# Seven instead of six gate tiles in the first phase of a fused LayerNorm, SSM and SwiGLU kernel, with its transposes through one PSUM bank

## The chip, the cores and the metric

The kernel runs on one core of one Trainium2 chip. The metric is the device time of one execution in microseconds (us); lower is better. A run of the kernel before takes about 180 us.

Engine names follow the profile: PE is TensorE, ACT is ScalarE, DVE is VectorE, POOL is GpSimd, SP is SyncE. ACTq and SPq are the sequencers of ScalarE and SyncE when they issue DMA loads. Times of a profile are counted from the start of its span. The span is about 1.7 us shorter than the device time.

## The reference, cut to what matters

The input is 2048 tokens of 512 bf16 values. They are layer-normalised; the result goes through a linear recurrence (the SSM part) and through a SwiGLU block with 1376 hidden columns; both are added to the input.

```python
def _layernorm(x, axis=-1, eps=1e-5):
    m = jnp.mean(x, axis=axis, keepdims=True)
    v = jnp.var(x, axis=axis, keepdims=True)
    return (x - m) / jnp.sqrt(v + eps)

def _B_ref(x, w_gate, w_up, w_down):        # w_gate, w_up: 512 x 1376
    g = _silu(x @ w_gate)
    u = x @ w_up
    return (g * u) @ w_down

xn = _layernorm(x, axis=-1)
return x + _A_ref(xn, ...) + _B_ref(xn, w_gate, w_up, w_down)   # _A_ref: the recurrence; cut
```

The hidden columns make ten full tiles of 128 and a rest of 96. Tokens are taken in four chunks of 512; a chunk is four token tiles of 128.

## The kernel before: the parts that matter

The kernel records each operation as a task with its reads and writes. A list scheduler puts the tasks into one fixed order for each engine, and semaphores are placed from the dependencies. Every engine then works through its order strictly in sequence. Keep that in mind: a computing instruction that waits holds up those behind it on its engine (VectorE's wait of 0.77 us in the profile after is the case that matters here).

The loads. `x_load(a)` brings one token tile (128 KB). `wg_load` brings gate weights: a0 holds rows 0 to 255 of the weight, a1 and a2 the next 128 rows each, and each of them only the columns that the first phase needs (`FH0`, six tiles). The loads a0 and a1 are issued by ScalarE, behind a tiny one (`ld_touch`, 0.2 KB); all others are issued by SyncE.

```python
FH0 = 6 * 128
def wg_load(nm, k0, k1, **kw):
    return dma("ld_wg" + nm, wg[:, k0:k1, 0:FH0], wg_v[:, k0:k1, 0:FH0], [("wg", nm)], ...)

x_load(0)
x_load(1)
act_q = [dma("ld_touch", ..., eng="act")]
act_q.append(wg_load("a0", 0, 2, eng="act", order=(act_q[-1],)))
x_load(2)
act_q.append(wg_load("a1", 2, 3, eng="act", order=(act_q[-1],)))
wg_load("a2", 3, 4)
x_load(3)
# ... parameters, the rest of the weights, token tiles 4 to 7
```

The layer norm of the first four token tiles, on VectorE except for one square root per tile on ScalarE.

```python
def ln_chunk0():
    last = ln_stat0(0, (bn_full(0),))
    last = bn_half(1, 0, order=(last,))           # statistics of tile 1, first half
    for a in range(4):
        last = g.add("dve", ... reciprocal of sd0[a] ..., order=(last,))
        for h in range(2):
            last = ln_half(a, h, order=(last,))   # normalised token tile, halves of 256
        if a < 3:
            last = bn_half(a + 1, 1, order=(last,))
            last = ln_stat0(a + 1, (last,))
        if a < 2:
            last = bn_half(a + 2, 0, order=(last,))
```

The transposes and the gate matmuls. A normalised half tile is transposed on PE into PSUM, the memory that PE writes its results to (two transposes). ScalarE then evacuates it, that is, copies it out to SBUF, the memory that PE reads, as `xnT`. In the kernel before, the two halves of a tile use the two banks of one PSUM pair, and six gate tiles use three more pairs, so all eight banks are taken. The gate matmuls of this phase have only 128 tokens each ("quarter matmuls").

```python
def xt_tile_fine(a, hs=(0, 1)):
    for h in hs:
        slot = xt_pair[0] + h                     # one bank for each half
        # PE: two transposes of xn_sb[:, a, half h] into ptr[:, slot, 0:256];
        #     with a == 3, h == 1 also that of 12 rows of parameters
        # ACT: evacuation to xnT[:, 0, a, 2h:2h+2, :]

def ffn_gate_quarters(pairs):                     # pairs = [0, 1, 2]: six gate tiles
    xt_pair[0] = next_pair()
    banks = {ip: next_pair() for ip in pairs}
    tiles = [(2 * ip + k, banks[ip] + k) for ip in pairs for k in range(2)]
    pe_warm(...)                                  # matmuls on constants
    ln_chunk0()
    # ... transposes of tile 0
    for q in range(4):                            # the four token tiles
        # ... for each gate tile 4 quarter matmuls (contraction 4 x 128);
        #     the transposes of tile q + 1 in between
    act_table(AF.Silu, (hold["evac"],))           # an activation that loads the Silu table
    for ip in pairs:
        silu_pair(0, ip, banks[ip])               # ACT, two gate tiles at a time
```

After the phase, PE goes on with matmuls of 512 tokens: `ffn_up(0, 0)` to `ffn_up(0, 2)`, then the gate tiles 6 to 9, and so on.

## Time and profile before

| kernel before | value | view of the profile |
|---|---|---|
| device time | 179.89 us, median of 3 runs (179.84 to 180.25) | list of runs |
| span | 178.2 us | page |
| first gate matmul | 5.89 us | timeline of PE |
| first up matmul, start of the 512-token stream | 12.65 us | timeline of PE |
| PE idle between these two ("holes") | 0.67 us | start-to-start distances of PE's instructions above 56 ns |
| token tile 1 landed | 3.96 us | last completion record of its load |

These are two lines of the page. The first gives busy time, share of the span and instructions of each engine, the second the chain of waits that ended last, by engine:

```profile
PE 174.2 (98%) x918; PEld 83.5 (47%) x926; DVE 162.0 (91%) x278; ACT 89.4 (50%) x117; POOL 9.6 (5%) x21
PE 95%; DMA 1%; DVE 1%; issue 1%; ACT 0%
```

PE is busy nearly all the time and is nearly all of the chain. This change can't make a busy PE faster, since it adds no gate work and removes none. It can only gain where PE idles, and that is in the first 12.65 us.

This is the timeline of PE in the phase (start in us, busy us, engine, line of the kernel, operation, output and inputs, shapes, count; in brackets idle time before it and what ended it):

```profile
5.89 1.17 PE L786 MATMUL pb<-xnT,wg 128*128 128x128 bf16 x18 [0.17 <-ACT xnT L571]
6.89 0.28 PE L565 MATMUL pb<-ident,xn_sb 128*128 128x128 bf16 x2
7.00 0.33 PE L786 MATMUL pb<-xnT,wg 128*128 128x128 bf16 x3
7.17 0.28 PE L565 MATMUL pb<-ident,xn_sb 128*128 128x128 bf16 x2
7.28 1.20 PE L786 MATMUL pb<-xnT,wg 128*128 128x128 bf16 x15
8.45 0.28 PE L565 MATMUL pb<-ident,xn_sb 128*128 128x128 bf16 x2
...
12.65 0.59 PE L738 MATMUL pb<-xnT,wu 128*128 128x512 bf16 x2
```

L786 are the quarter matmuls, L565 the transposes. Busy times overlap, since matmuls are pipelined; use the starts. From 7.28 to 8.45 there are 1.17 us for 15 matmuls, which at 56 ns take 0.84 us: here PE idles 0.33 us although the lines show no wait: 0.19 us of it is inside the group, before the matmul at 7.64 us, and 0.13 us between its last matmul and the transposes at 8.45 us.

The following lines are VectorE's timeline at the start:

```profile
3.09 0.69 DVE L525 BATCH_NORM_STATS2 st<-x_sb 128x6 f32<-128x512 bf16 x1 [3.09 <-DMA x_sb<-in_A_x_dram]
3.81 0.18 DVE L517 BATCH_NORM_AGGREGATE mv<-st 128x2 f32<-128x6 f32 x1
3.99 0.43 DVE L507 BATCH_NORM_STATS2 st<-x_sb 128x6 f32<-128x256 bf16 x1
4.36 0.16 DVE L529 RECIPROCAL rstd<-sd 128x1 f32<-128x1 f32 x1
4.56 0.60 DVE L512 TENSOR_SCALAR xn_sb<-x_sb,mv,rstd 128x256 bf16<-128x256 bf16 x2
```

ScalarE's end of the phase is its load of the Silu table and then the silus:

```profile
11.53 1.28 ACT L461 ACT_TABLE_LOAD   x1
12.83 0.29 ACT L461 ACTIVATE sm<-epst 128x1 f32<-128x1 f32 x1
13.03 2.83 ACT L750 ACTIVATE sg<-pb 128x1024 bf16<-128x1024 f32 x3
```

The last view of before is that of the DMA issues in the first 12 us: output and source, sequencer, count, KB of one, and the median time from issue to landing in us.

```profile
x_sb<-in_A_x_dram SPq DMA_DIRECT2D x4, 128.0 KB, 3.3
wg<-in_B_w_gate_dram ACTq DMA_DIRECT2D x1, 384.0 KB, 3.6
```

### The profile page before, as it was taken

What the parts mean: (1) busy time and instruction counts of PE and PEld (TensorE: products, weight loads), DVE (VectorE), ACT (ScalarE), POOL (GpSimd) and SP (SyncE); (2) the same over time, 40 slices, a digit from 0 to 9 for tenths busy, and PEclk for the clock granted to TensorE, in tenths of its full rate; (3) what the DMA queues carried; (4) which work ended last, traced back from release to release, by engine and by line L of the source; (5) the groups of instructions that cost most, each with busy time, mean ns of one, the idle gap of its engine ahead of it and who ended that gap; (6) DMA issues with size and microseconds to landing.
All of it is one profiled execution on the core that took longest, in us unless ns stands there. A gap on an engine that the chain in (4) does not pass through costs nothing.

```text
span 178.2 us, 2394 instructions
## 1 busy us (share of the span) xinstructions
PE 174.2 (98%) x918; PEld 83.5 (47%) x926; DVE 162.0 (91%) x278; ACT 89.4 (50%) x117; POOL 9.6 (5%) x21
## 2 busy tenths in 40 slices
PE   8999999999999999999999999999999999999994
PEld 3784444444444444444444444444444444444743
DVE  2959983889799999999999999999999999999983
ACT  4479989999799948016565651000965620000000
POOL 3033100002200000040000000000000000000000
PEclk9999999999999999999999999999999999999999
DMA  5995569459360000002420000001100000000122
GB/s 170 364 339 117 120 118 115 97 169 346 95 118 4 0 0 0 0 18 72 95 56 0 0 0 4 0 0 59 58 0 4 0 0 0 0 0 4 59 86 91
DMA packets 22979, 12.37 MB, mean 69 GB/s; under 512 B 15193, under 2 KB 22969, under 8 KB 22969
## 3 DMA queue, kind: packets, MB, share of 16 engines
q1 hardware_dynamic: 22472, 11.64, 24.7%
q10 hardware_dynamic: 496, 0.59, 1.0%
q8 instruction: 7, 0.11, 0.3%
q14 instruction: 4, 0.02, 0.0%
HBM read 6.46 MB, written 2.10 MB: 48 GB/s over the span
## 4 chain that ended last, share of the span: by engine, by line
PE 95%; DMA 1%; DVE 1%; issue 1%; ACT 0%
PE pb L738 36%; PE pb L938 21%; PE pb L855 16%; PE pb L951 15%; PE pb L786 3%; PE pb L818 2%; DMA x_sb<-in_A_x_dram 1%; PE pb L828 1%; PE pb L565 1%; DVE st L525 0%; DVE st L507 0%; ACT xnT L571 0%; DVE xn_sb L512 0%; DVE x_sb L956 0%; DVE mv L517 0%
## 5 line engine op out<-in xcount | busy, mean ns | idle before, releaser
L895 DVE TENSOR_TENSOR_SCAN rot<-sm,car,rot 128x512 bf16<-128x512 f32 x32 | 39.0, 1266 | 0.1
L938 PE MATMUL pb<-wd,hT 128*128 128x512 bf16 (+3 forms) x194 | 38.1, 355 | 0.2
L738 PE MATMUL pb<-xnT,wu 128*128 128x512 bf16 x160 | 37.3, 379 | 0.0
L738 PE MATMUL pb<-xnT,wg 128*128 128x512 bf16 x136 | 32.0, 379 | 0.0
L951 PE MATMUL pb<-W,hss 128*128 128x512 bf16 (+2 forms) x140 | 28.1, 355 | 0.2
L855 PE MATMUL pb<-xnT,BT 128*128 128x512 bf16 x128 | 28.1, 379 | 0.0
L938 PEld LDWEIGHTS pb<-wd,hT 128*128 128x128 bf16 (+1 forms) x198 | 18.5, 98 | 19.9
L738 PEld LDWEIGHTS pb<-xnT,wu 128*128 128x128 bf16 x160 | 15.5, 98 | 18.8 <-ACT uf L808 0.4
L808 ACT ACTIVATE uf<-pb 128x1024 bf16<-128x1024 f32 x20 | 20.4, 1027 | 7.0 <-PE pb L738 6.2
L750 ACT ACTIVATE sg<-pb 128x1024 bf16<-128x1024 f32 x20 | 20.2, 1023 | 7.3 <-PE pb L738 7.3
L738 PEld LDWEIGHTS pb<-xnT,wg 128*128 128x128 bf16 x136 | 13.1, 98 | 16.4 <-issue 0.8
L951 PEld LDWEIGHTS pb<-W,hss 128*128 128x128 bf16 x144 | 13.5, 98 | 14.3
L855 PEld LDWEIGHTS pb<-xnT,BT 128*128 128x128 bf16 x128 | 12.5, 98 | 15.1
L862 ACT ACTIVATE u_sb<-pb 128x1024 bf16<-128x1024 f32 x16 | 16.4, 1026 | 4.6 <-PE pb L855 4.2
L810 DVE TENSOR_TENSOR hT<-sg,uf 128x1024 bf16<-128x1024 bf16 x20 | 13.5, 682 | 1.0 <-ACT uf L808 0.8
L886 DVE TENSOR_TENSOR rot<-u_sb,cosT 128x2048 bf16<-128x2048 bf16 x8 | 9.7, 1217 | 2.9 <-ACT cosT L699 2.9
L956 DVE TENSOR_TENSOR x_sb<-pb,x_sb 128x512 bf16<-128x512 f32 (+2 forms) x18 | 10.8, 622 | 1.4 <-PE pb L951 1.4
L837 ACT ACTIVATE sg<-pb 96x1024 bf16<-96x1024 f32 x2 | 2.0, 1020 | 17.3 <-PE pb L818 17.3
L501 ACT ACTIVATE xn_sb<-x_sb,nmr,rstd 128x512 bf16<-128x512 bf16 x8 | 5.9, 804 | 9.5 <-DVE nmr L498 9.5
L886 DVE TENSOR_TENSOR rot<-rot,cosT 128x2048 bf16<-128x2048 bf16 x8 | 9.7, 1216 | 0.1
L886 DVE TENSOR_TENSOR rot<-rot,sin 128x2048 bf16<-128x2048 bf16 x8 | 9.7, 1217 | 0.0
L886 DVE TENSOR_TENSOR rot<-u_sb,sin 128x2048 bf16<-128x2048 bf16 x8 | 9.7, 1215 | 0.0
(77 smaller groups left out, 141.2 us busy)
## 6 DMA issues: line engine op xcount, KB each, us to landing
out_dram<-x_sb SPq DMA_DIRECT2D x15, 128.0 KB, 1.7
x_sb<-in_A_x_dram SPq DMA_DIRECT2D x3, 512.0 KB, 7.6
wd<-in_B_w_down_dram SPq DMA_DIRECT2D x1, 1280.0 KB, 7.1
wu<-in_B_w_up_dram SPq DMA_DIRECT2D x1, 768.0 KB, 4.8
wg<-in_B_w_gate_dram SPq DMA_DIRECT2D x1, 608.0 KB, 6.2
wu<-in_B_w_up_dram SPq DMA_DIRECT2D x1, 608.0 KB, 7.3
x_sb<-in_A_x_dram SPq DMA_DIRECT2D x4, 128.0 KB, 3.3
wg<-in_B_w_gate_dram ACTq DMA_DIRECT2D x1, 384.0 KB, 3.6
```

What stands on the lines that cost most here:

```text
L501: g.add("act", lambda e, a=a: e.activation(out=xn_sb[:, a % NXN, :], in_=x_sb[:, a, :], func=AF.Identity, scale=rstd[:, a:a + 1], bias=nmr ...
L738: inst = e.matmul(pbank[0:fs, bk, :].rearrange("p (j t) -> p j t", j=4), lhsT=w[:, kt, i * 128:i * 128 + fs], rhs=xnT[:, c % 2, :, kt, :], ...
L750: g.add("act", lambda e: e.activation(out=sg[rows, sl, 0:n, :].rearrange("p a t -> p (a t)"), in_=pair_f32(rows, bk, 512 * n), func=AF.Sil ...
L808: g.add("act", lambda e: e.activation(out=uf[rows, ul, 0:n, :].rearrange("p a t -> p (a t)"), in_=pair_f32(rows, bk, 512 * n), func=AF.Ide ...
L810: g.add("dve", lambda e: e.tensor_tensor(out=hT[rows, hb, i0:i0 + n, :], in0=sg[rows, sl, 0:n, :], in1=uf[rows, ul, 0:n, :], op=ALU.mult), ...
L855: inst = e.matmul(pbank[:, bk, :].rearrange("p (j t) -> p j t", j=4), lhsT=BT[:, ri, kt, pt * 128:(pt + 1) * 128], rhs=xnT[:, c % 2, :, kt ...
L862: g.add("act", lambda e: e.activation(out=u_sb[:, us].rearrange("p r t -> p (r t)"), in_=pair_f32(slice(0, 128), b0), func=AF.Identity), r ...
L886: tt = lambda out, a, b, op, r, w, nm: g.add("dve", lambda e: e.tensor_tensor(out=out, in0=a, in1=b, op=op), reads=r, writes=w, name="%s_% ...
L895: g.add("dve", lambda e, A0=A0, A1=A1, k=k, ri=ri, pt=pt: e.tensor_tensor_scan(out=A1[:, k, ri, :], data0=rr[:, pt:pt + 1].to_broadcast([1 ...
L938: inst = e.matmul(pbank[:, bk, 0:nc_], lhsT=hT[0:fs, hb, i, lt * 128:(lt + 1) * 128], rhs=wd[0:fs, i, c0:c0 + nc_], start=(i == 0), stop=F ...
L951: inst = e.matmul(pbank[:, bk, 0:nc_], lhsT=hss[:, hb, pt, ri, lt * 128:(lt + 1) * 128], rhs=W12[:, ri, pt, c0:c0 + nc_], start=False, sto ...
L956: g.add("dve", lambda e, bk=bk, a=a, c0=c0, nc_=nc_: e.tensor_tensor(out=x_sb[:, a, c0:c0 + nc_], in0=pbank[:, bk, 0:nc_], in1=x_sb[:, a, ...
```

## The change

The intent is to fill PE's holes. VectorE needs about 1.74 us for the layer norm of a token tile, while PE's share for it is 24 quarter matmuls and 4 transposes, 28 x 56 ns = 1.57 us. With a seventh gate tile it is 32 x 56 ns = 1.79 us. The seventh tile needs a PSUM bank, so both halves of a tile's transposes now share one bank, and an eighth gate tile, made with 512-token matmuls, takes that bank at the end. The four silus then have all eight banks, and the first up matmul must wait for the first silu. So that it needn't wait long, token tile 3 is evacuated by VectorE, and ScalarE loads its Silu table earlier. The gate loads ahead of the phase grow from 768 to 896 columns, 128 KB in all. The diff, cut to its core:

```diff
         FH0 = 6 * 128
+        NQ = 7
+        FG = NQ * 128
@@ wg_load and ld_wg1
-    return dma("ld_wg" + nm, wg[:, k0:k1, 0:FH0], wg_v[:, k0:k1, 0:FH0], ...)
+    return dma("ld_wg" + nm, wg[:, k0:k1, 0:FG], wg_v[:, k0:k1, 0:FG], ...)
-        dma("ld_wg1", wg[:, :, FH0:Fh], wg_v[:, :, FH0:Fh], ...)
+        dma("ld_wg1", wg[:, :, FG:Fh], wg_v[:, :, FG:Fh], ...)
@@ ln_chunk0: order on VectorE
-                for h in range(2):
-                    last = ln_half(a, h, order=(last,))
+                last = ln_half(a, 0, order=(last,))
                 if a < 3:
                     last = bn_half(a + 1, 1, order=(last,))
                     last = ln_stat0(a + 1, (last,))
+                last = ln_half(a, 1, order=(last,))
                 if a < 2:
                     last = bn_half(a + 2, 0, order=(last,))
@@ xt_tile_fine: one bank, tile 3 evacuated by VectorE
-                slot = xt_pair[0] + h
+            slot = xt_pair[0]
...
+            if a == 3:
+                t = g.add("dve", lambda e: e.tensor_copy(out=dst, in_=src), ..., order=(hold["xn3"],))
+                if par:
+                    g.add("dve", lambda e: e.tensor_copy(out=praw..., in_=ptr[:, slot, 512:524]), ..., order=(t,))
+            else:
+                t = g.add("act", lambda e: e.activation(out=dst, in_=src, func=AF.Identity), ...)
@@ ffn_gate_quarters
-            xt_pair[0] = next_pair()
             banks = {ip: next_pair() for ip in pairs}
+            xt_pair[0] = tiles.pop()[1]
...
+                for k0, k1 in ((0, 2), (2, 3), (3, 4)) if q == 0 else ((0, 2), (2, 4)):
+                    if k0 == 2 and q < 3:
+                        xt_tile_fine(q + 1, 0)
+                    for i, bk in tiles:
+                        # ... quarter matmuls k0 to k1 of gate tile i
+                if q < 3:
+                    xt_tile_fine(q + 1, 1)
...
+            seq = ["sd0", "ev00", "sd1", "ev01", "ev10", "sd2", "ev11", "sd3", "ev20", "ev21"]
+            # ... this order is fixed on ScalarE
-            act_table(AF.Silu, (hold["evac"],))
+            act_table(AF.Silu, (hold["ev21"],))
+            ffn_mm(0, NQ, "g", xt_pair[0])
@@ order of the first chunk
-        ffn_gate_quarters([0, 1, 2])
+        ffn_gate_quarters([0, 1, 2, 3])
...
-        for ip in range(3, 5):
-            ffn_gate(0, ip)
+        ffn_gate(0, 4)
```

## The prediction

> **What bounds the kernel.** TensorE. The page gives PE 174.2 of 178.2 us (98%), and 95% of the chain that ended last is PE; the granted clock is 1.0. Read one by one, matmuls of 512 columns start 216 ns apart, those of 128 columns 56 ns apart. This agrees with the Trainium skill, "TensorE: Matmul & The Clock Gate", section "Wait — 56ns, not 53.3ns?" (55.6 and 215.7 ns warm). From 12.65 us, where the 512-column stream starts, to the last matmul I find no wait beyond places where records are missing. VectorE is busy 91%, but off the chain.
>
> So the only time to win is before 12.65 us. The timeline of PE between the first gate matmul (5.89) and 12.65 shows holes: 0.19 us at 7.6, 0.13 at 8.4, 0.17 at 10.2, 0.15 around the parameter transpose at 10.6; sum 0.63. The cause is VectorE: one token tile of layernorm takes it 1.74 us (xn tiles start at 4.56, 6.30, 8.04, 9.78), while PE's share for six gate tiles is 24 matmuls and 4 transposes, 28 x 56 ns = 1.57 us.
>
> **What the change does.**
> - A seventh gate tile makes PE's share 32 x 56 ns = 1.79 us: 16 added quarter matmuls (0.89 us) partly fill the holes, and four 512-column matmuls (0.86 us) go later. PE work in total is unchanged; only filled holes count. Ceiling: 0.63 - 0.15 (parameters stay), about 0.45 us.
> - One transpose bank costs a round trip. In before, from a transpose to the first matmul after its evacuation is 0.75 us (6.89 to 7.64). Between transposes stand 14 matmuls, 0.78 us, so this mostly fits. At the start it doesn't: the second half's transpose waits for the first evacuation, and the first gate matmul comes at about 6.0, 0.1 later.
> - The fourth square root is ordered before tile 2's first evacuation on ScalarE and waits for its statistics: about 0.15 us of PE idle.
> - 128 KB more gate weight is loaded ahead of the tokens. At the 371-389 GB/s of the windows this delays token tile 2 (landed 5.57, needed at 5.66) by an estimated 0.2, hence the statistics by 0.1-0.15.
> - The early Silu table load (1.28 us, measured) and two evacuations on VectorE free ScalarE: the first silu (before: 13.03) needs only tile 1's last matmul, about 12.8-13.0. All eight banks hold gate tiles, so the first up matmul must wait for that silu (1.0 us): ready at about 14.1, when tile 7's 512-column matmuls (0.86 us) end at 14.1-14.3.
>
> Sum: up starts at about 14.2, against 12.65 + 8 x 0.216 = 14.37 with two gate tiles counted ahead. Gain 0.2 us, all on the critical path. The last VectorE scan result lands 0.35 us before PE uses it (168.4 against 168.74), which caps a gain near 0.35.
>
> **Prediction: 179.68 us, range 179.30 to 180.10; faster by over 2% 0.01, same 0.98, slower 0.01.**
>
> **What will show it.** Timeline of PE: first quarter matmul at 6.0; tile 7's 512-column matmuls from about 13.3; first up matmul 14.1-14.3; holes in the phase below 0.45 us; PE unbroken after. ScalarE: table load at about 10.4, four silus in a row from 13.0.
>
> **What would make it wrong.** The first up matmul waiting over 0.2 us on the silu; a late token tile; a hole at every single-bank transpose; PE waiting for VectorE at the last hss, which would hide a larger gain.

## The result, and the profile after

| | before, same rounds | after |
|---|---|---|
| median device time | 180.07 us (179.84 to 180.46, 6 runs) | 180.19 us (179.72 to 180.32, 6 runs) |
| ratio after/before | | 1.000, 95% interval 0.9982 to 1.0018: same |
| span of the profiled run | 178.2 us | 178.6 us |
| first gate matmul | 5.89 us | 6.75 us |
| from it to the first up matmul | 6.76 us | 8.09 us |
| first up matmul | 12.65 us | 14.84 us |
| holes in between | 0.67 us | 0.26 us |
| token tile 1 landed | 3.96 us | 4.76 us |

Ratios lie within 0.001 of the ratio of the mean times of the same rounds (`after_one_ring` excepted), and aren't quite the ratio of the medians that are quoted. The kernel before itself took 180.07 us in these rounds; at the time of the prediction 179.89 us was known. The profiled run of after took 180.30 us, the profiled one of before 179.93 us; the two traces therefore show one of after's longer runs beside one of before's shorter runs, and their difference of 0.37 us in span is larger than that of the kernels.

The page's line of busy time for the kernel after; PE is still the busiest, a little less so over a longer span:

```profile
PE 173.3 (97%) x929; PEld 83.9 (47%) x937; DVE 162.3 (91%) x281; ACT 88.7 (50%) x114; POOL 9.9 (6%) x21
```

The timeline of PE in the phase, L780 being the quarter matmuls and L739 the 512-token matmuls:

```profile
5.80 0.27 PE L565 MATMUL pb<-ident,xn_sb 128*128 128x128 bf16 x2 [1.41 <-DVE xn_sb L514]
5.91 0.49 PE L474 MATMUL pb<-const-bfloat16-1.0 128*128 128x256 bf16 x3
6.63 0.27 PE L565 MATMUL pb<-ident,xn_sb 128*128 128x128 bf16 x2 [0.23 <-ACT xnT L577]
6.75 0.94 PE L780 MATMUL pb<-xnT,wg 128*128 128x128 bf16 x14
7.53 0.28 PE L565 MATMUL pb<-ident,xn_sb 128*128 128x128 bf16 x2
7.64 0.94 PE L780 MATMUL pb<-xnT,wg 128*128 128x128 bf16 x14
8.42 0.27 PE L565 MATMUL pb<-ident,xn_sb 128*128 128x128 bf16 x2
...
13.98 1.03 PE L739 MATMUL pb<-xnT,wg 128*128 128x512 bf16 x4
14.84 1.46 PE L739 MATMUL pb<-xnT,wu 128*128 128x512 bf16 x6
```

Now the transposes come every 0.89 us (6.63, 7.53, 8.42), and 14 matmuls and 2 transposes at 56 ns are 0.896 us. PE has no holes here; the aim of the change is met. Two gate tiles more now come before the first up matmul: sixteen quarter matmuls, which are as much work as four matmuls of 512 tokens, and the four of tile 7. Counted as eight matmuls of 512 tokens they cost 8 x 0.216 = 1.73 us that before has to do later. So the stretch from first gate to first up takes 8.09 - 1.73 = 6.36 us against 6.76 us: the change wins 0.40 us there.

But the phase begins 0.86 us later. VectorE's timeline tells why:

```profile
3.10 0.69 DVE L527 BATCH_NORM_STATS2 st<-x_sb 128x6 f32<-128x512 bf16 x1 [3.10 <-DMA x_sb<-in_A_x_dram]
3.83 0.18 DVE L519 BATCH_NORM_AGGREGATE mv<-st 128x2 f32<-128x6 f32 x1
4.78 0.43 DVE L509 BATCH_NORM_STATS2 st<-x_sb 128x6 f32<-128x256 bf16 x1 [0.77 <-DMA x_sb<-in_A_x_dram]
5.12 0.15 DVE L531 RECIPROCAL rstd<-sd 128x1 f32<-128x1 f32 x1
5.31 0.35 DVE L514 TENSOR_SCALAR xn_sb<-x_sb,mv,rstd 128x256 bf16<-128x256 bf16 x1
```

Token tile 0 is there as early as before (3.10 against 3.09). Then VectorE waits 0.77 us for token tile 1, whose first-half statistics stand in its order ahead of tile 0's reciprocal. The tile that PE needs next is held up by one that it needs 1.7 us later (PE transposes them at 5.80 and 7.53 us). The view of DMA issues has the same (median of four token tiles 4.1 instead of 3.3 us):

```profile
x_sb<-in_A_x_dram SPq DMA_DIRECT2D x4, 128.0 KB, 4.1
wg<-in_B_w_gate_dram ACTq DMA_DIRECT2D x1, 448.0 KB, 4.5
```

The completion records of that load add a detail: a load here ends with 16 updates, as many as the core has DMA engines. For token tile 1, fifteen of them were in at 4.17 us in the kernel after, and the sixteenth came at 4.76 us; in the five loads that landed next, the last update again came 0.45 to 0.70 us behind the fifteenth. This looks like one late DMA engine, but the records don't name the engine. In the kernel before, the last two updates came at 3.92 and 3.96 us.

ScalarE's end of the phase:

```profile
11.01 1.28 ACT L463 ACT_TABLE_LOAD   x1
12.31 0.29 ACT L463 ACTIVATE sm<-epst 128x1 f32<-128x1 f32 x1
13.62 1.94 ACT L751 ACTIVATE sg<-pb 128x1024 bf16<-128x1024 f32 x2 [1.02 <-PE pb L780]
```

The table is ready 1 us before the first silu can start, and the first silu (about 1.02 us) is done at 14.64 us, ahead of PE's end of tile 7 at 14.84 us. No wait is left here.

After the first up matmul nothing changes: from it to the last matmul the kernel after takes 161.37 us, the kernel before 163.20 - 1.73 = 161.47 us.

### The profile page after: what moved, and what is told of

The parts are those of the page before. It is cut to its first block, busy times and chain, and to the rows that moved or that the text cites. A ratio compares the mean times of both kernels' runs of the same rounds, so it can differ in the third digit from the quotient of the medians.

```text
span 178.6 us, 2421 instructions
## 1 busy us (share of the span) xinstructions
PE 173.3 (97%) x929; PEld 83.9 (47%) x937; DVE 162.3 (91%) x281; ACT 88.7 (50%) x114; POOL 9.9 (6%) x21
## 4 chain that ended last, share of the span: by engine, by line
PE 95%; DMA 2%; DVE 1%; issue 1%; SPq 0%; ACT 0%
PE pb L739 35%; PE pb L937 21%; PE pb L854 15%; PE pb L950 15%; PE pb L780 4%; DMA x_sb<-in_A_x_dram 2%; PE pb L817 2%; PE pb L827 1%; PE pb L565 1%; DVE st L509 0%; SPq L400 0%; ACT xnT L577 0%; DVE xn_sb L514 0%; DVE x_sb L955 0%; PE pb L562 0%
## 5 line engine op out<-in xcount | busy, mean ns | idle before, releaser
L739 PE MATMUL pb<-xnT,wu 128*128 128x512 bf16 x160 | 37.3, 379 | 0.0
L739 PE MATMUL pb<-xnT,wg 128*128 128x512 bf16 x132 | 31.3, 379 | 0.0
L739 PEld LDWEIGHTS pb<-xnT,wu 128*128 128x128 bf16 x160 | 15.6, 98 | 18.9 <-issue 0.2
L739 PEld LDWEIGHTS pb<-xnT,wg 128*128 128x128 bf16 x132 | 12.7, 98 | 15.7 <-issue 0.8
```

Source lines behind the costliest of these rows:

```text
L739: inst = e.matmul(pbank[0:fs, bk, :].rearrange("p (j t) -> p j t", j=4), lhsT=w[:, kt, i * 128:i * 128 + fs], rhs=xnT[:, c % 2, :, kt, :], ...
```

## The experiments

Four explanations stood against each other, and the expectations refer to them by content:

- **Loads.** The 128 KB of added gate weight, on ScalarE's queue beside SyncE's, delays token tile 1 and so the start.
- **Chance.** When token tile 1 lands varies from run to run whatever the kernel, and the one profile of after happened to be late.
- **One bank.** The single transpose bank costs at the start and at each transpose.
- **A later chain.** PE is held later by something else, and what the phase gains is given back there.

In the texts theory W is "Loads", theory S is "Chance" (there: a DMA engine that is late in some executions), theory D is "A later chain", and theory E is its opposite: only the start matters.

All kernels gave correct results. In those that move a task, the move is made after the schedule is fixed, or the size that the scheduler sees is left as it was, so the orders on the compute engines stay what they were; exceptions are named. "Ratio" is to the kernel before of the same rounds.

### Both kernels again

No edit. `before_again` and `after_again` are the two kernels, run and profiled once more on one chip.

> Control: the same program as before. Theory W (weights): the 128 KB of gate weight more is what made token tile 1 land at 4.76 us in the profile of after (3.96 in that of before); then before lands near 3.96 again and its times form one group near 179.9. Theory S (straggler): in some executions of either kernel one of the DMA engines delivers its share 0.3 to 0.7 us late; then the ten times of this program spread over two groups about 0.4 us apart (179.9 and 180.4), ratio to before 1.000 within 0.002.

> Control: the same program as after. Theory W: token tile 1 lands at 4.6 to 4.8 us again and the first up matmul starts at 14.7 to 14.9, ratio to before 1.000 to 1.003. Theory S: where no engine is late, tile 1 lands at about 4.05, the first gate matmul at 6.0 and the first up matmul at 14.1 to 14.2; the times spread over two groups as those of before do, each about 0.2 us lower; ratio 0.9985 to 0.9995.

Measured: before_again 180.11 us (5 runs), ratio 0.9995 [0.9983, 1.0007]. after_again 179.87 us (5 runs), ratio 0.9981 [0.9968, 0.9993]. Means: 179.90 us for after against 180.19 us for before's 11 runs, so here after is 0.28 us faster, where the first series had no difference (means 180.12 and 180.12). The profile of after_again fell on its slowest run (180.21 us; the others 179.71 to 179.90), and it shows the late tile again:

```profile
4.71 0.43 DVE L509 BATCH_NORM_STATS2 st<-x_sb 128x6 f32<-128x256 bf16 x1 [0.76 <-DMA x_sb<-in_A_x_dram]
```

What follows: the late landing isn't a single accident, but the profiles of after have twice fallen on runs slower than its median. The phase itself is steady: 8.09 us in both profiles of after, holes 0.26 and 0.28 us. In before_again token tile 2 landed at 6.03 instead of 5.57 us, and the holes were 0.88 instead of 0.67 us. Before has its own sensitivity to late loads, one tile further on. Of the expectations neither came whole: tile 1's landing at 4.68 us was as theory W had it, the ratio of 0.998 close to that of theory S, and before's times showed no two groups.

### Only the larger loads, and only the smaller ones

`six_big_loads` is before with after's loads: six gate tiles, 896 columns loaded ahead. `seven_small_loads` is after with 768 columns ahead and the seventh tile's 128 columns in a load of their own behind a2.

```diff
# six_big_loads, against before (the size hint to the scheduler stays)
-  wg[:, k0:k1, 0:FH0], wg_v[:, k0:k1, 0:FH0]
+  wg[:, k0:k1, 0:FG],  wg_v[:, k0:k1, 0:FG]        # FG = 7 * 128
-  dma("ld_wg1", wg[:, :, FH0:Fh], ...)
+  dma("ld_wg1", wg[:, :, FG:Fh], ...)
# seven_small_loads, against after
-  wg[:, k0:k1, 0:FG],  wg_v[:, k0:k1, 0:FG]
+  wg[:, k0:k1, 0:FH0], wg_v[:, k0:k1, 0:FH0]
   wg_load("a2", 3, 4)
+  dma("ld_wga3", wg[:, :, FH0:FG], wg_v[:, :, FH0:FG], [("wg", "a3")], 0)
```

> Before with the larger gate loads alone (896 instead of 768 columns ahead of the tokens), the order on every engine else unchanged. Theory W: tile 1 lands 0.5 to 0.8 us later than in before (4.5 to 4.8), the first gate matmul at 6.4 or later, the first up matmul at 13.2 to 13.5 instead of 12.65, time +0.5 us (ratio 1.003). Theory S: tile 1 lands at most 0.15 later than 3.96 when no engine is late, up at 12.75 to 12.85, ratio 1.000 to 1.001.

> After with the gate loads of before (768 columns) ahead of the tokens, and the seventh tile's 128 columns as a load of its own (128 KB in rows of 256 bytes) between the last of them and token tile 3. Theory W: tile 1 lands at 3.96, first up matmul at 14.1, ratio to before 0.9975, 0.5 us below after. Theory S: little differs from after in the mean (within 0.15 us); the extra load may land after 6.7 us, which would put a hole before the seventh tile's first matmul.

Measured: six_big_loads 180.30 us (6 runs), ratio 1.0011 [0.9997, 1.0026]. Its first gate matmul is at 6.28 us, 0.39 us later than in before, for the same reason as in after:

```profile
4.42 0.43 DVE L508 BATCH_NORM_STATS2 st<-x_sb 128x6 f32<-128x256 bf16 x1 [0.48 <-DMA x_sb<-in_A_x_dram]
```

seven_small_loads 180.75 us (6 runs), ratio 1.0033 [1.0016, 1.005]. Token tile 1 landed at 4.44 us although only 768 columns were loaded beside it. Its phase is the shortest of all kernels with seven tiles (8.02 us, holes 0.20 us), and yet it is the slowest of the four kernels of these rounds, partly through a wait near 50 us, to which I come below.

What follows: the larger loads by themselves may cost about 0.2 us, but the interval just includes nothing. The smaller loads didn't bring the early start back. So the size of the loads alone doesn't decide when tile 1 lands; the loads theory in its simple form is not shown.

### All loads from one queue

The gate loads a0 and a1 move from ScalarE's to SyncE's sequencer, in the order x0, x1, a0, x2, a1, a2, x3. With that, token tile 1 has no competitor. Done for both kernels.

```diff
+        for nm, behind in (("ld_wga0", "ld_x1"), ("ld_wga1", "ld_x2")):
+            t = next(t for t in streams["act"] if t.name == nm)
+            streams["act"].remove(t)
+            t.eng = "sp"
+            streams["sp"].insert(next(k for k, s in enumerate(streams["sp"]) if s.name == behind) + 1, t)
```

> After with all early loads on SyncE's queue, token tile 1 ahead of the gate weights (x0, x1, wg a0, x2, wg a1, wg a2, x3), orders of all compute engines unchanged. Theory W (the gate weights of ScalarE's queue take the bandwidth that token tile 1 needs, and the larger ones of after more so): x1 lands at 3.4 to 3.6 us instead of 4.7, first gate matmul at 5.95 to 6.1 instead of 6.7, first up matmul at 14.05 to 14.25 instead of 14.8, time 0.5 to 0.7 us below after. Theory S (an engine is late now and then, whatever the order): the first gate matmul stays at 6.4 to 6.8 in the profile, and the mean time within 0.15 us of after.

> Before with the same reordering of loads. In before x1 landed at 3.96 and was asked for at 3.99, so an earlier x1 buys nothing at tile 1. Theory W: first gate matmul 5.85 to 5.95, first up matmul 12.6 to 12.7, time within 0.15 us of before (up to 0.2 lower where x2 and x3 came late). Theory S: the same, with the same two groups of times.

Measured: before_one_ring 181.82 us (6 runs), ratio 1.009 [1.0075, 1.0105]. after_one_ring 181.60 us (6 runs, 179.99 to 183.57); ratio 1.0111 [1.0071, 1.015], but two of the six (182.90 and 183.57) are slow, and the mean of the other four, 181.07 us, is 1.005 of before's 180.16 us. before_one_ring is slower, and after_one_ring is in three of its four fast runs, where theory W expected a gain of 0.5 to 0.7 us over after, and both theories next to no change for before. Token tile 1 does land early, at 3.35 and 3.40 us, which shows the competition; VectorE no longer waits for it. But the loads behind it suffer. The view of DMA issues in the first 12 us has 2.98 MB at a mean of 249 GB/s for before_one_ring, and 3.52 MB at 293 GB/s for before. The load of token tiles 4 to 7 was issued 0.99 us later (6.71 instead of 5.72 us) and landed 3.2 us later (17.06 instead of 13.88 us). Token tiles 8 to 11 then landed at 42.52 instead of 40.43 us, and this stops PE, by way of VectorE and ScalarE; these are groups of waits (engine, line that waits, releaser, us in total, times, longest; of the second line's two waits, the shorter one of 3.5 us is meant):

```profile
PE pb L738 <- ACT uf L808: 2.1, 1, 2.1
ACT xn_sb L501 <- DVE nmr L498: 11.7, 2, 8.2
```

What follows: there is a second chain that can bound this kernel. The DMA transposes of the parameter matrices go one after the other, then token tiles 8 to 11 are loaded, VectorE makes their statistics, GpSimd the reciprocal roots, ScalarE normalises them, and only behind that in its order does it evacuate the up tile that PE waits for, at 50 to 52 us. Where PE is held there, it goes on 9.50 to 9.98 us after those token tiles have landed, so no single distance can be given. In before that is a wait of 0.09 us at 50.09 us, in seven_small_loads of 0.47 us, counted from start to start, at 50.6 us (its tiles landed at 41.15 us), in after and after_again nothing. The profile of after_one_ring fell on its fastest run (179.99 us), where this chain held PE by only 0.10 us (at 50.16 us), so what its longer runs waited for isn't seen.

### Six gate tiles through one bank

`six_one_bank` is after with `NQ = 6`, so with VectorE's new order, tile 3 on VectorE and the early table, but without the seventh tile. The transposes get a bank pair of their own. Here the scheduler was left free.

```diff
-        NQ = 7
+        NQ = 6
-            xt_pair[0] = tiles.pop()[1]
+            xt_pair[0] = next_pair()
+            reserved.add(xt_pair[0])
-            ffn_mm(0, NQ, "g", xt_pair[0])
-        ffn_gate_quarters([0, 1, 2, 3])
+        ffn_gate_quarters([0, 1, 2])
```

> After without its seventh tile: six gate tiles in quarters and the loads of before, but one transpose bank in halves, VectorE's new order, tile 3 evacuated by VectorE, early Silu table. If it is the seventh tile that fills PE's holes (as I predicted, with VectorE's 1.74 us per token tile as the limit): holes between first gate and first up matmul 0.6 us or more, first up at 12.65 to 12.95. If it is VectorE's new order that takes the holes away (1.6 us per tile in the profiles of after, where statistics stand between the halves, against 28 x 56 ns = 1.57 us): holes below 0.4, first gate at 6.0, first up at 12.35 to 12.55, time 0.2 to 0.5 us below before.

Measured: 181.12 us (5 runs), ratio 1.0056 [1.0044, 1.0068]. The timeline of PE:

```profile
6.37 0.27 PE L565 MATMUL pb<-ident,xn_sb 128*128 128x128 bf16 x2 [0.23 <-ACT xnT L577]
6.48 0.83 PE L781 MATMUL pb<-xnT,wg 128*128 128x128 bf16 x12
7.21 0.27 PE L565 MATMUL pb<-ident,xn_sb 128*128 128x128 bf16 x2
7.32 0.83 PE L781 MATMUL pb<-xnT,wg 128*128 128x128 bf16 x12
8.04 0.27 PE L565 MATMUL pb<-ident,xn_sb 128*128 128x128 bf16 x2
...
14.18 2.10 PE L739 MATMUL pb<-xnT,wu 128*128 128x512 bf16 x9 [0.76 <-ACT sg L751]
```

Two things. First, the wait of 0.76 us at 14.18 us (0.92 us counted from start to start) is a flaw of my variant: its bank order makes the first up matmul wait for the first silu. It makes the total useless as a price of the seventh tile. Second, the phase can be read. Without that wait the holes are 0.72 us, about as much as in before. Transposes come every 0.84 us (6.37, 7.21, 8.04), where 12 matmuls and 2 transposes need only 14 x 56 ns = 0.784 us: the bank is written, evacuated by ScalarE and free again after 0.84 us here. With 14 matmuls the PE work of 0.896 us just covers this.

But apart from 0.15 us around the parameters these holes aren't those of before. Four of 0.06 us are round trips of the single bank, and 0.32 us before the transposes at 9.98 us comes from ScalarE, whose fixed order has the fourth square root, waiting for VectorE, ahead of an evacuation:

```profile
9.27 0.29 ACT L521 ACTIVATE sd<-mv,epst 128x1 f32<-128x1 f32 x1 [0.54 <-DVE mv L519]
```

What follows: the seventh tile is what makes a single bank free of cost in the phase, and it covers most of the wait for the fourth square root. That it also fills the holes of before isn't shown by this run. In VectorE's new order a tile takes 1.60 us here (normalised from 5.04 and from 6.64 us) instead of 1.74 us, and six gate tiles need 1.57 us of PE. So the new order alone, with six tiles and two banks, might have filled most of before's holes; that variant was not run.

### The Silu table late again

`late_table` is after with tile 3 and the parameters evacuated by ScalarE again, and the Silu table loaded behind them.

```diff
+        at = next(k for k, s in enumerate(streams["act"]) if s.name == "xTev2_1") + 1
+        for k, nm in enumerate(("xTev3_0", "xTev3_1", "parTev")):
+            # the task moves from VectorE's to ScalarE's order, as an activation with Identity
+            streams["act"].insert(at + k, t)
```

> After with tile 3 and the parameters evacuated by ScalarE again, and the Silu table loaded behind them, all other orders unchanged. If the early table is needed because all eight banks hold gate tiles: table load at 13.1 instead of 11.0 (first gate matmul at 6.7), first silu at 14.6 to 14.8, first up matmul 15.6 to 15.9 instead of 14.8, time 0.8 to 1.1 us above after. If the silu is not on the path there, within 0.15 us of after.

Measured: 180.66 us (5 runs), ratio 1.003 [1.0018, 1.0042], on average 0.54 us above before of its rounds. By the two ratios that is about 0.9 us (0.0049 of 180 us) above after_again. PE now waits for the first silu:

```profile
15.09 1.24 PE L742 MATMUL pb<-xnT,wu 128*128 128x512 bf16 x5 [0.73 <-ACT sg L754]
```

What follows: the early table, with tile 3's evacuations on VectorE that make room for it, is a needed part of the change. Without the two the gain is more than lost.

### Token tiles 8 to 11 earlier

Is the gain given back on the second chain? In `after_x8_early` and `before_x8_early` the load of token tiles 8 to 11 is issued before three of the DMA transposes instead of behind them.

```diff
+        x8 = named["ld_x8"]
+        streams["sp"].remove(x8)
+        streams["sp"].insert(streams["sp"].index(named["xTd1"]), x8)
```

> After with token tiles 8 to 11 loaded before instead of behind three of the DMA transposes, orders of all compute engines unchanged. Theory D (a second chain, from the serial DMA transposes over the load of tiles 8 to 11, VectorE's statistics, ScalarE's normalising, to an up evacuation near 50 us, caps what PE gains: in the traces PE waits there unless it comes at least 9.66 us after that load has landed): tiles 8 to 11 land at 26 us instead of 39 to 41, never a PE wait near 50, mean time 0.15 to 0.4 us below before (ratio 0.998 to 0.999) and a spread under 0.5 us. Theory E (only the start, the landing of token tile 1, makes the spread and eats the gain): ratio and spread as in after, 0.998 to 1.000.

> Before with the same earlier load. Theory D: the wait of 0.09 us near 50 us in the profile of before goes, mean time 0.05 to 0.2 us below before, spread smaller. Theory E: within 0.05 us of before.

Measured: after_x8_early 179.85 us (5 runs, 179.60 to 180.13), ratio 0.9985 [0.9973, 0.9998]; before_x8_early 180.05 us (5 runs), ratio 0.9998 [0.9985, 1.001]. Before gains nothing that can be measured (means 180.05 and 180.11 us), and after is where after_again was. So there is no sign that the second chain eats the gain in usual runs, though the expectations of the two theories lie too close together for this pair to decide it alone.

This pair gives the best comparison of the change itself, because token tile 1 happened to land at nearly the same time in both: 4.24 us and 4.20 us. Their first up matmuls are at 14.42 us and 12.84 + 1.73 = 14.57 us. And after has a handicap here that the profile shows. These are its last warm-up matmuls of 256 columns:

```profile
5.45 0.78 PE L474 MATMUL pb<-const-bfloat16-1.0 128*128 128x256 bf16 x3
```

They take 0.78 us, where the same three took 0.49 us in the profile of after (the line at 5.91 us): their starts are 213 ns apart instead of 108 ns. PE was still at half speed, in the transposes before them too, so the first evacuation came later, and the first gate matmul came 2.09 us after tile 1 landed instead of 1.99 us.

### Token tiles first

`after_x8_tokens_first` is after_x8_early with two more moves. The activation that loads the Sqrt table goes ahead of the gate loads in ScalarE's order, meant to hold these loads back, and a2 goes behind token tile 3 and the parameters.

```diff
+        warm = next(t for t in act if t.name == "act_warm")
+        act.remove(warm)
+        act.insert(1, warm)
+        sp.remove(a2)
+        sp.insert(sp.index(named["ld_lre"]) + 1, a2)
```

> The earlier load of tiles 8 to 11, and at the start the four token tiles first: SyncE's queue x0 to x3, parameters, last gate slice; ScalarE's queue the touch, then the Sqrt table load, then gate slices a0 and a1, issued 1.5 us later than in after. Theory W: x1 lands at 3.4 to 3.6, so tile 0 is normalised at 4.55 and the first gate matmul comes at 6.0 (or when a0 lands, 5.8 to 6.2); first up at 14.1 to 14.3; time 0.4 to 0.7 us below after, ratio to before 0.9955 to 0.9975. If a0 now lands too late (over 6.5) the gain is lost again. Theory S: an engine comes late all the same, x1 over 4.

Measured: 179.84 us (5 runs, 179.58 to 179.97), ratio 0.9982 [0.9968, 0.9996], mean 179.79 us against 180.11 us. It is the fastest kernel by a hair, but not by its design: the gate loads weren't held back. ScalarE's timeline shows them issued at 1.30 us, in the middle of the table load that stands before them in its order:

```profile
1.23 1.28 ACT L463 ACT_TABLE_LOAD   x1 [1.23 <-PEq L1069]
1.30 0.93 ACTq L400 DMA_DIRECT2D wg<-in_B_w_gate_dram  x2
```

Token tile 1 landed at 4.19 us, so the expected early start didn't come. My expectation was missed.

### The first gate load held back

`after_a0_later` repairs that: the issue of a0 also waits for a memset of GpSimd, which ends near 2.1 us.

```diff
+        next(t for t in act if t.name == "ld_wga0").deps.add(next(t for t in streams["pool"] if t.name == "car0"))
```

> As after_x8_tokens_first, whose gate slices were not held back (issued at 1.30 and 1.74 us although a table load stood before them), and now a0's issue really waits: for GpSimd's last small memset, which ended at 2.09 us in the profile of after. Theory W (the gate weights on the other queue take the bandwidth of token tile 1): a0 issued at 2.15 to 2.3, x1 lands at 3.35 to 3.6 as on one queue, so tile 0 is normalised at 4.55, first gate matmul at 5.95 to 6.1 (6.2 if TensorE is still cold), first up matmul at 14.05 to 14.3, a0 lands at 5.2 to 5.8, the second chain undisturbed (tiles 4 to 7 landed by 14.0), ratio to before 0.9965 to 0.998. Theory S (an engine is late whatever competes): x1 at 4.0 or later, first gate matmul 6.2 or later, ratio as of after_x8_tokens_first, 0.998 to 0.999. A third outcome: a0 lands after 6.0 and becomes what the first gate matmul waits for.

Measured: 180.52 us (6 runs, 179.95 to 181.37), ratio 1.0013 [0.9997, 1.0029]; the means are 180.57 and 180.18 us. The profile fell on the slowest run. Token tile 1 landed at 3.31 us, and VectorE took it up at 3.96 us without a wait. So a competing load is what keeps this tile from landing at 3.3 us. So the early start of theory W didn't come; the third outcome did: a0 landed at 6.42 us and became what the first gate matmul waits for. What I hadn't expected is the second wait, for a2, which landed at 9.12 us, its last update again about 0.9 us behind the fifteenth.

```profile
6.47 0.96 PE L780 MATMUL pb<-xnT,wg 128*128 128x128 bf16 x14 [0.26 <-DMA wg<-in_B_w_gate_dram]
9.17 0.56 PE L780 MATMUL pb<-xnT,wg 128*128 128x128 bf16 x7 [1.24 <-DMA wg<-in_B_w_gate_dram]
```

What follows: at the start, token tiles and gate weights share one supply. Holding one back turns its wait into one for the other.

### All profiles side by side

This table collects the start of every profile in which it can be read, in us. "Tile 1" is the landing of token tile 1, "columns" the width of the gate loads ahead of the phase.

| kernel | columns | tile 1 | first gate matmul | holes |
|---|---|---|---|---|
| before | 768 | 3.96 | 5.89 | 0.67 |
| before_again | 768 | 3.97 | 5.97 | 0.88 |
| before_x8_early | 768 | 4.20 | 6.08 | 0.68 |
| six_one_bank | 768 | 4.49 | 6.48 | 0.72 |
| seven_small_loads | 768 + 128 | 4.44 | 6.54 | 0.20 |
| six_big_loads | 896 | 4.40 | 6.28 | 0.69 |
| late_table | 896 | 4.09 | 6.18 | 1.07 with the wait for the silu |
| after_x8_tokens_first | 896 | 4.19 | 6.17 | 0.38 |
| after_x8_early | 896 | 4.24 | 6.33 | 0.26 |
| after_again | 896 | 4.68 | 6.67 | 0.28 |
| after | 896 | 4.76 | 6.75 | 0.26 |
| after_one_ring | one queue | 3.35 | 6.21 | 0.39 |
| before_one_ring | one queue | 3.40 | 5.91 | 0.68 |
| after_a0_later | a0 held back | 3.31 | 6.47 | 1.58 with the wait for a2 |

Two readings. First, where tile 1 is late, the first gate matmul follows it at a nearly fixed distance: in before's structure 1.88 us (4.20 to 6.08, 4.40 to 6.28), in after's 1.98 or 1.99 us (4.19 to 6.17, 4.49 to 6.48, 4.68 to 6.67, 4.76 to 6.75), and 2.09 or 2.10 us in the three profiles in which PE was still at half speed at the first transposes (late_table, after_x8_early, seven_small_loads; warm-up matmuls 213 ns apart). The difference between before and after at full speed, 0.11 us, is the price of the single bank: the second half's two transposes have to wait for the first evacuation, so they now stand between it and the first gate matmul (6.63 and 6.75 us in after), and two transposes take 2 x 56 ns. Second, with the loads competing, tile 1 landed at 3.96 to 4.49 us (mean of five 4.21) with 768 columns, and at 4.09 to 4.76 us (mean of six 4.39) with 896. The ranges overlap; eleven profiles don't settle whether the 0.18 us between the means is the added weight or chance.

## Why the prediction was right or wrong

**Right:** I gave 0.98 to a change within 2%, and the ratio was 1.000. That tests little: the ceiling that I gave, 0.45 us, is far below 2% (3.6 us). The gain of 0.2 us that I predicted did not show in the first series (mean difference 0.00 us). In the repetition it was 0.28 us, and 22 runs of before (6, 11 and the 5 of before_again) against 11 of after, pooled over the two series, give a mean difference of 0.13 us, with a standard error of about 0.08 us. That this is near 0.2 us is partly luck: two errors, a larger gain in the phase and a later start, work against each other, as shown below. The median of 180.19 us lies just above the top of my range, 180.10 us. Before was 0.18 us slower in these rounds than the 179.89 us on which the range was built.

**What bounds the kernel: right.** PE is 97% busy in the profile after. After the first up matmul, 161.4 us pass in before, after and both repetitions, to within 0.1 us.

**The holes: right in size.** I predicted less than 0.45 us; 0.26 us are left, and without the seventh tile 0.72 us (six_one_bank), though mostly from other causes than in before. That it is the added work, and not in part VectorE's new order (1.60 instead of 1.74 us for a tile), that filled before's holes is argued and not shown.

**The single bank: right in kind, near in size.** Predicted 0.1 us at the start; measured 0.11 us. The round trip is 0.84 us rather than the 0.75 us that I read from before, so the 0.896 us of PE work between transposes covers it with little to spare.

**The fourth square root's order: right in kind.** Predicted 0.15 us of PE idle; a hole of 0.10 us stands at 10.30 us in after, behind a square root that waited 0.48 us for VectorE.

**The early table and the wait for the silu: right.** The table load came at 11.01 us and the silus at 13.62 us, against 10.4 and 13.0 predicted; both are 0.6 us late, somewhat less than the 0.75 us by which the phase started later than predicted. There was no wait for the silu, and late_table shows one of 0.73 us without this part.

**The start: wrong, and this is the step that failed.** The prediction says "the first gate matmul comes at about 6.0, 0.1 later", from the single bank alone. It came at 6.75 us in after and at 6.67, 6.33 and 6.17 us in the repetition and the two variants that load token tiles 8 to 11 earlier. I had seen that more weight is loaded ahead of the tokens, but charged it to token tile 2 ("an estimated 0.2"), which in after landed at 6.33 us and was taken up at 6.36 us without a wait. "A late token tile" stood on my list of what would make the prediction wrong, but I hadn't asked which one. The tile that matters is tile 1, because VectorE's order puts its first-half statistics ahead of tile 0's reciprocal, and before had just 0.03 us of slack there. The sum for the profiled run: tile 1 0.80 us later, less the 0.05 us by which before wasn't held by it (5.89 - 3.96 = 1.93 us instead of 1.88), plus 0.11 us for the bank, is the 0.86 us by which the phase starts later. The phase gives back 0.40 us, and the first up matmul, corrected by 1.73 us, is 0.46 us later than in before.

**At an equal start the change gains an estimated 0.29 us** (0.40 - 0.11). The pair with token tile 1 at 4.24 and 4.20 us agrees: the first up matmul is 0.15 us earlier, with 0.04 us of the tile and 0.10 us of a slow PE clock against it, and the means of their runs are 0.22 us apart (179.83 and 180.05 us).

**What stays open.** Landing times are seen only in profiled runs, so how late tile 1 is on average in the others isn't known. Whether after's late landings (4.76 and 4.68 us) come from the 128 KB or from chance is not settled. Why the last update lags through a series of loads is not shown by any run. The most direct test of the start, a variant of after with tile 1's first statistics behind tile 0's reciprocal on VectorE, was not run, and neither was VectorE's new order with six tiles in two banks. I also can't say what held the longer runs of after_one_ring.

**Where the Trainium skill bears on this.** "TensorE: Matmul & The Clock Gate", section "Wait — 56ns, not 53.3ns?", gives 55.6 and 215.7 ns between starts of warm matmuls of 128 and 512 columns; the traces agree with 56 and 216 ns, and every sum above rests on them. The same page, section "What's actually happening", says that the array runs at half speed at first and that the moment of the change varies from run to run, as its window is free-running. The traces agree: 256-column warm-up matmuls were 213 ns apart up to about 5.9 us in after_x8_early, while in after the 512-column ones had gone from 427 to 220 ns apart by 3.9 us. "DMA: Bandwidth & Descriptors", section "Issuing engines are not separate DMA queues", says that loads issued by different engines share the same 16 DMA engines and interleave. The landing of token tile 1 agrees: 3.31 to 3.40 us without a competitor, 3.96 to 4.76 us with gate weights from the other queue. Had I applied that sentence to tile 1, I would have asked what waits for it.

## What to carry to other kernels

When a change adds bytes ahead of a phase, look up the first consumer of every load that shares the DMA engines with them, and look in the in-order queues for work of a later tile that stands before work of an earlier one: a slack of 0.03 us there is a warning. A change that fills holes on the bounding engine is worth only what is left after the start of that phase; compare phases at equal starts, and compare starts over several profiles, because landing times here moved by 0.8 us. Give a gain of 0.2 us to repeated rounds and not to two profiles, which can fall on a fast run of one kernel and a slow run of the other.

## What the Trainium skill lacked or had wrong

- "DMA: Bandwidth & Descriptors", section "Issuing engines are not separate DMA queues", says that starting DMAs from several engines saves only the sequencer's time to initiate them. With all loads on SyncE's queue, 249 GB/s were moved in the first 12 us instead of 293 GB/s, and a load issued 0.99 us later landed 3.2 us later (before_one_ring). So more was lost here than the issue time. That the second queue by itself makes the difference isn't shown: the order of the loads changed too, and 1.27 us of the 3.2 us is the distance of that load's last update from its fifteenth.
- The same page has nothing on the last of a load's 16 updates lagging through a whole series of plain loads issued by SyncE and ScalarE: 0.59 us on the load of token tile 1 in after, about 0.9 us on a2 in after_a0_later.
- "ScalarE: Activation LUTs", section "What ACT_TABLE_LOAD costs", gives 1283 ns for the load, which agrees (1.28 us), and about 1380 ns more for a drain, 2.66 us in total. No such drain is seen here: in after the load starts at 11.01 us and the next activation at 12.31 us, 1.30 us later, and the activation before the load had ended at 10.99 us.
- No page says in so many words that DMA issues behind a table load in ScalarE's order are not held up by it. The nearest is "PSUM — Partial Sum Buffer", section "Engine vs sequencer instructions", which says of a nop that the sequencer waits for the instructions before it to be dispatched and not to complete. In after_x8_tokens_first two gate loads were issued from 1.30 us, during a table load that ran from 1.23 to 2.51 us.
- "PSUM — Partial Sum Buffer", section "PSUM bank collisions raise a hardware error ⚠️", says that accesses to a bank have to be guarded by semaphores. It doesn't say what the round trip of such a wait costs: 0.84 us from one pair of transposes to the next with a ScalarE evacuation of 128 x 256 in between (six_one_bank).
